# k' of four pairs of token tiles and all of q' as seven products of quarters, with a table for VectorE's and ScalarE's order

## The chip, the cores and the metric

The kernel runs on one core of a Trainium2 chip. The metric is the device time of one execution in microseconds. Before the change three runs took 728.2, 730.2 and 730.42 us; the median is 730.2.

## The reference, cut to what matters

Token matrix `x` is 2048 x 576, in float32. Two branches are mixed by a gate `g` of each token:

```python
g = sigmoid((x * gate_w).sum(-1, keepdims=True))
# branch a: linear attention, 32 heads of 18
q, k, v = split(x @ wqkv)
phi = lambda t: where(t > 0, t + 1, exp(t)) + 1e-6
kv  = einsum("bhsd,bhse->bhde", phi(k), v)
z   = phi(k).sum over tokens
o   = einsum("bhqd,bhde->bhqe", phi(q), kv) / (einsum("bhqd,bhd->bhq", phi(q), z) + 1e-6)
a   = o @ wo
# branch b: real part of a 2-D DFT, by four matrix products
b = Cr @ (x @ Wr.T) - Ci @ (x @ Wi.T)
out = g * a + (1 - g) * b
```

## The kernel before

There are 16 token tiles of 128 rows (`NT`), and 8 pairs of them (tile p and p + 8). A matrix product is done with fp32r operands in three passes: each operand is split in a high part (ScalarE, `hi_of`, L176) and a low part (VectorE, `lo_of`, L186), and TensorE sums high x high, high x low and low x high. The depth of 576 is four chunks of 128 and a rest of 64, whose low part shares a chunk with its high part; so one 128 x 288 half of a tile takes 4 x 3 + 2 = 14 matmuls (`steps`, L272).

The work in order of time:

1. k. Four tiles are done together while the first data arrive (L488 to L503), then twelve one by one in two halves (`k_half`, L452). A raw tile of x is loaded by SP (`load_next`, L256) and split (`split_next`, L262). Each half is turned into its feature by two ScalarE instructions and one of VectorE (`feature`, L341 to L345), and each tile is then split (`k_split`, L462).
2. x'·k, over all tokens, in 5 chunks x 16 tiles (L617 to L672). Into it go the loading and splitting of the token tiles, the sum z, and the product with v (`kv_step`).
3. q, 16 tiles one by one (`q_tile`, L677), the gate's column with them. Between the tiles stand the building of k'v, its product with `wo` to a 576 x 576 matrix M (`build_m`, L762), the moving of M's rows into chunks by DMA from POOL's queue (`move_m`, L771), M's splitting (`split_m`, L787), the division by the denominators (`normalise`, L696) and the forms of the DFT weights (`right`, L402).
4. The transposed q times M, 16 tiles x 2 halves x 14 matmuls (L1109 to L1118).
5. Branch b in two rounds (from 262 us): `Hidden.run`, then `sequence`. Both use Winograd's scheme: a product of 2 x 2 blocks with seven block products instead of eight, on sums of blocks. `PRODUCTS` (L81) says which sum of the left quarters (A22, A11, A12 and four sums, in the order of the code) meets which of the right. The left forms of x are made by `Left` (L352) a few at a time during steps 1 to 4 and stored in DRAM.

Order: TensorE's, VectorE's, ScalarE's and SP's instructions run in the order in which the code issues them (`manual_schedule`; TensorE's order is fixed so only from step 5 on). Every engine waits at the head of its own queue for its data.

Of the kernel before, what the change touches and what calls it, by code (L numbers as in the profile page):

```python
# [8 lines left out]
F = mybir.dt.float32  # L9
# [20 lines left out]


# [3 lines left out]

def gsize(g):  # L50
    return min(GW, D - g * GW)
# [3 lines left out]


# [8 lines left out]

TPAIR = 2 * 7 * HALF * 4
XD = 2 * D * 4
# [6 lines left out]
WH, WL = 5 * HALF * 4, 4 * HALF * 4  # L74
QH = HALF, HALF + 2


LAY_Q = dict(xs=(-256, 4864, 9984, 43776), hi=(15104, 20864), lo=(26688, 31296))
# [3 lines left out]
ORDER = (3, 2, 7, 6, 1, 4, 5)  # L82
MIX_AT = ACC_AT
# [7 lines left out]

# [43 lines left out]
def kernel(  # L135
# [6 lines left out]
    wq: bass.AP,  # L142
    wv: bass.AP,
# [14 lines left out]

    def at(offset, shape, dtype=F, name="t"):
        count[0] += 1  # L160
        t = nc.alloc_sbuf_tensor_at(f"{name}_{count[0]}", list(shape), dtype,
                                    offset=base + offset)
        return t.ap()
# [15 lines left out]
    pending, paced = [], ExitStack()  # L179

# [64 lines left out]
    acc = [at(ACC_AT + i * D * 4, [P, D], F, "acc") for i in range(NT)]  # L245


    raws, split = [], []
    order = []
    xs_ring = Ring(0, 0, 0)  # L250

    def new_xs(name="xs", ring=xs_ring):
        o = ring.next()
        return (at(o, [P, 10, P], R, name), at(o + XS // 2, [P, 5, P], F, "xraw"))

    def load_next():  # L256
        if order:
            xs, raw = new_xs()
            nc.sync.dma_start(out=raw, in_=xa[order.pop(0)])
            raws.append((xs, raw))  # L260
# [8 lines left out]
    def x_at(lay):  # L269
        xs_ring.at, xs_ring.n = [SLOT_AT + o for o in lay["xs"]], 0  # L270
# [10 lines left out]
    def split_wide(t, c, raw):  # L281
        hi_of(t[:, c], raw)
        if c < KC:
            lo_of(t[:, 5 + c], raw, t[:, c])
        else:
            lo_of(t[64:, c], raw[64:], t[64:, c])

    rest_ring = Ring(CONST_AT + 3584, 1184, 2)

    class Wide:  # L290


        def __init__(self, src, lay, start=SLOT_AT, widths=(HALF, HALF)):
            self.src, self.lay, self.got = src, lay, {}
            self.start, self.widths = start, widths

        def load(self, h, pieces=(KC,), queues=None, also=lambda k: None):

            n = self.widths[h]
            cols = slice(h * HALF, h * HALF + n)  # L300
            hi = at(self.start + self.lay["hi"][h], [P, 5, n], R, "wd")
            los, c = [], 0
            for k in pieces:
                o = self.start + self.lay["lo"][h] + c * n * 4
                los.append((c, at(o, [P, k, n], R, "wd"), at(o, [P, k, n], F, "wraw")))
                c += k
            rest = at(rest_ring.next(), [P, n], F, "wraw")
            self.got[h] = hi, los, rest
            queues = queues or [nc.sync] * (len(pieces) + 1)
            for i, (c, _, raw) in enumerate(los):  # L310
                also(i)
                queues[i].dma_start(out=raw, in_=self.src[:, c:c + raw.shape[1], cols])
            also(len(los))
            queues[-1].dma_start(out=rest, in_=self.src[:, KC, cols])

        def split(self, h, n=1, lo_of=lo_of):

            hi, los, rest = self.got[h]
            for c, lo, raw in los:
                k = lo.shape[1]  # L320
                m = max(k * n // KC, 1)
                for a in range(0, k, k // m):
                    cs = slice(a, a + k // m)
                    hs = slice(c + a, c + a + k // m)
                    hi_of(hi[:, hs], raw[:, cs])
                    lo_of(lo[:, cs], raw[:, cs], hi[:, hs])
                    yield
            hi_of(hi[:, KC], rest)
            lo_of(hi[64:, KC], rest[64:], hi[64:, KC])
            yield  # L330

        def row(self, h, j):
            hi, los = self.got[h][:2]
            if j <= KC:
                return hi[:, j]
            return next(lo[:, j - 5 - c] for c, lo, _ in los if c <= j - 5 < c + lo.shape[1])


    es = Ring(Y_AT, 1184, 3)

    def feature(dst, ps):  # L341
        e = at(es.next(), [P, HALF], F, "e")
        nc.scalar.activation(e, ps, AF.Relu, scale=-1.0)
        nc.scalar.activation(e, e, AF.Exp, scale=-1.0)  # L344
        nc.vector.scalar_tensor_tensor(dst, ps, 0.0, e, op0=ALU.max, op1=ALU.add)  # L345


    xforms = [scratch([P, 7, 2, 2 * P], "xm") for _ in range(NP)]
    xrest = scratch([NP * 96, 7 * P], "xr")
    xrest_of = xrest.rearrange("(g q j r) n -> g j r q n", g=2, q=4, j=3)  # L350

    class Left:  # L352

        def __init__(self, k, start, after):
# [922 lines left out]
```

## Time and profile before

| what | value |
|---|---|
| three runs | 728.2, 730.2, 730.42 us |
| span of the profiled execution, first to last instruction | 727.9 us |
| TensorE busy | 723.1 us, 5446 matmuls |
| VectorE busy | 600.3 us, 994 instructions |
| ScalarE busy | 335.5 us, 521 instructions |
| GpSimd busy | 57.1 us, 98 instructions |
| DMA | 158.83 MB, 218 GB/s |

Besides its span, the profiled execution has no time of its own on record; what lies around the span is read from the runs. In the rows, PE is TensorE and PEld its weight loads, DVE is VectorE, ACT is ScalarE, POOL is GpSimd, SP issues DMAs. A row of a group has the line of the code, the engine, the operation, output and inputs with their shapes, the count, then the busy time in us and the mean time of one in ns, then the idle time of the engine just before, with what ended most of it. Many instructions have the line of a helper (L176, L186, L196, L206).

### The profile page before, as it was taken

To read this page: it belongs to the slowest core of one execution; us is meant where nothing else is said; L and a number is where in the kernel's file an instruction comes from. 1 tells how busy PE (TensorE), PEld (TensorE's weight loads), DVE (VectorE), ACT (ScalarE), POOL (GpSimd) and SP (SyncE) were. 2 spreads that over 40 slices of the span, in tenths; PEclk is the share of its full clock that TensorE was granted. 3 is DMA by queue.
4 is the path that set the end of the run, shared out by engine and by line. 5 is a ranking of instruction groups with operands and counts; after the bars stand their busy time and mean duration, and the time that the engine had idled before them with its cause. 6 is when DMAs were issued, how large, how long until landed. Compare 5 with 4: busy or idle time off the path is not lost.

```text
span 727.9 us, 13874 instructions
## 1 busy us (share of the span) xinstructions
PE 723.1 (99%) x5446; PEld 722.0 (99%) x5446; DVE 600.3 (82%) x994; ACT 335.5 (46%) x521; POOL 57.1 (8%) x98
## 2 busy tenths in 40 slices
PE   9999999999999999999999999999999999999997
PEld 9999999999999999999999999999999999999997
DVE  5689877689999948989989989857889988788884
ACT  6898346678643544453434333323435322232330
POOL 1011300051132110000000000000000000000000
PEclk9999999999999999999999999999999999999999
DMA  7376796676477999644475666889954443544440
GB/s 255 91 274 220 266 332 199 221 219 230 147 257 279 365 331 380 182 163 144 147 263 168 225 233 199 306 281 402 377 206 135 168 148 124 163 151 140 152 152 33
DMA packets 54228, 158.83 MB, mean 218 GB/s; under 512 B 6412, under 2 KB 10828, under 8 KB 53140
## 3 DMA queue, kind: packets, MB, share of 16 engines
q1 hardware_dynamic: 44916, 118.90, 48.2%
q0 software_dynamic: 8960, 38.65, 14.6%
q8 instruction: 43, 0.70, 0.4%
q10 hardware_dynamic: 288, 0.41, 0.2%
q14 instruction: 21, 0.17, 0.1%
HBM read 115.06 MB, written 41.39 MB: 215 GB/s over the span
## 4 chain that ended last, share of the span: by engine, by line
PE 99%; DVE 0%; DVEq 0%; issue 0%; POOL 0%; POOLq 0%
PE bank L1051 49%; PE bank L206 23%; PE bank L896 14%; PE bank L626 8%; PE bank L502 2%; PE bank L731 1%; PE bank L232 1%; PE bank L608 0%; DVE row L1067 0%; PE bank L611 0%; DVE ys L196 0%; DVEq L1275 0%; POOL ones_f L228 0%; POOL ident masks.py:197 0%; DVEq L1067 0%
## 5 line engine op out<-in xcount | busy, mean ns | idle before, releaser
L1051 PE MATMUL bank<-fh,c 128*128 128x288 f32 x1792 | 357.4, 295 | 0.0
L1051 PEld LDWEIGHTS bank<-fh,c 128*128 128x128 f32 x1792 | 287.3, 188 | 0.1
L1051 PE MATMUL bank<-fl,c 128*128 128x288 f32 x896 | 264.3, 295 | 0.0
L176 ACT ACTIVATE c<-craw 128x1792 fp32r<-128x1792 f32 (+1 forms) x84 | 121.6, 1447 | 188.2 <-DVE craw L196 167.5
L1051 PEld LDWEIGHTS bank<-fl,c 128*128 128x128 f32 x896 | 168.9, 188 | 0.3
L186 DVE TENSOR_TENSOR c<-craw,c 128x1792 fp32r<-128x1792 f32 (+4 forms) x86 | 142.0, 1654 | 2.8 <-ACT c L176 2.6
L196 DVE TENSOR_TENSOR craw<-craw 128x256 f32<-128x256 f32 (+1 forms) x192 | 98.4, 513 | 24.2 <-DMA craw<-in_ci_dram 12.7
L206 PE MATMUL bank<-wd,xs 128*128 128x288 f32 (+1 forms) x784 | 105.9, 296 | 0.0
L206 PEld LDWEIGHTS bank<-wd,xs 128*128 128x128 f32 x784 | 104.6, 188 | 0.1
L896 PE MATMUL bank<-wf,xf 128*128 128x288 f32 x588 | 91.8, 296 | 0.0
L896 PEld LDWEIGHTS bank<-wf,xf 128*128 128x128 f32 x588 | 84.0, 189 | 0.0
L206 PE MATMUL bank<-mw,qs 128*128 128x288 f32 x448 | 63.2, 297 | 0.0
L626 PE MATMUL bank<-pk,c 128*128 128x288 f32 x448 | 60.8, 296 | 0.0
L206 PEld LDWEIGHTS bank<-mw,qs 128*128 128x128 f32 x448 | 59.9, 188 | 0.2 <-DVE qs L186 0.2
L626 PEld LDWEIGHTS bank<-pk,c 128*128 128x128 f32 x448 | 59.9, 189 | 0.0
L196 DVE TENSOR_TENSOR ys<-bank,ys 128x288 f32<-128x288 f32 x63 | 28.8, 457 | 17.1 <-PE bank L1051 14.0
L345 DVE SCALAR_TENSOR_TENSOR acc<-bank,e 128x288 f32<-128x288 f32 x64 | 28.2, 454 | 17.6 <-ACT e L344 12.2
L186 DVE TENSOR_TENSOR fl<-fl,fh 128x864 fp32r<-128x864 f32 (+1 forms) x32 | 34.7, 1094 | 6.7 <-ACT fh L176 5.4
L176 ACT ACTIVATE fh<-fl 128x864 fp32r<-128x864 f32 (+1 forms) x32 | 29.8, 949 | 16.3 <-DVE fl L196 16.3
L896 PE MATMUL bank<-wf,xr 96*128 96x288 f32 x112 | 33.3, 297 | 0.0
L1116 ACT ACTIVATE acc<-bank,gate 128x288 f32<-128x288 f32 x32 | 16.1, 502 | 35.0 <-PE bank L206 34.8
L196 DVE TENSOR_TENSOR ys<-ys,bank 128x288 f32<-128x288 f32 x47 | 21.2, 450 | 13.0 <-PE bank L1051 12.5
(107 smaller groups left out, 664.8 us busy)
## 6 DMA issues: line engine op xcount, KB each, us to landing
xf<-xm SPq DMA_DIRECT2D x42, 512.0 KB, 8.9
craw<-in_cr_dram SPq DMA_DIRECT2D x32, 512.0 KB, 4.0
craw<-in_ci_dram SPq DMA_DIRECT2D x32, 512.0 KB, 3.5
xraw<-in_xa_dram SPq DMA_DIRECT2D x28, 320.0 KB, 3.4
xm<-xb POOLq DMA_DIRECT2D x8, 1024.0 KB, 6.4
wf<-wm SPq DMA_DIRECT2D x14, 576.0 KB, 5.1
xr<-xr SPq DMA_DIRECT2D x14, 448.0 KB, 8.3
xm<-xb POOLq DMA_DIRECT2D x8, 768.0 KB, 5.8
```

The costliest lines, as they stand in the source:

```text
L176: return nc.scalar.activation(dst, src, AF.Copy, bias=bias)
L186: nc.vector.tensor_tensor(out=dst, in0=src, in1=hi, op=ALU.subtract)
L196: nc.vector.tensor_tensor(out=dst, in0=a, in1=b, op=op)
L206: nc.tensor.matmul(ps, a, b, start=(n == 0), stop=(n == len(pairs) - 1))
L232: nc.tensor.matmul(warm[:, :P], ones_f, ones_f, start=True, stop=True)
L345: nc.vector.scalar_tensor_tensor(dst, ps, 0.0, e, op0=ALU.max, op1=ALU.add)
L502: nc.tensor.matmul(ps[i], x[:, i * P:(i + 1) * P], wkt.row(h, j), start=(c == 0 and n == 0), stop=(c == KC and n == 1))
L626: nc.tensor.matmul(ps[h][:, :HALF], t[:, a, k], pk[s][:, b, half(h)], start=(s == 0 and n == 0), stop=(s == NT - 1 and n == len(passes) - 1))
L731: nc.tensor.transpose(banks[c // KC][:, (c % KC) * P:(c % KC + 1) * P], a, ident)
L896: nc.tensor.matmul(ps, a, b, start=(start and n == 0), stop=(n == len(ops) - 1), skip_group_check=True)
L1051: nc.tensor.matmul(ps[q], c[x][:, l, k], factors[p](y, f), start=(p == 0 and i == 0), stop=(p == NP - 1 and i == 2))
L1116: done.append(nc.scalar.activation(acc[i][:, half(h)], ps[:, :HALF], AF.Copy, scale=gate[:, i:i + 1]))
```

## The change

- k of tile pairs 4 to 7, and q of all eight pairs, are computed as seven products of quarters. A pair's x is a 2 x 2 matrix of quarters (tile p or p + 8; one half of the depth or the other, 256 of 288 rows of it), and so are the weights. A product is 2 chunks x 3 passes = 6 matmuls. The remaining 2 x 32 depth rows are added by two plain matmuls to each of the four outputs. So a pair takes 50 matmuls. k of pairs 0 to 3 stays plain, in two groups of four tiles.
- The left forms of x (`Left`) are those that branch b uses; k, q and branch b now take the same ones. The loads of single x tiles for k and q go away. x's quarters are loaded by SP's queue and no longer by POOL's. Pair 7's forms are read back from DRAM for q, pairs 0 and 1 stay for branch b.
- Sums of products are made in three ways: TensorE adds into a bank into which ScalarE has copied another (`copy`), TensorE goes on in a bank that was copied out, or VectorE adds a bank and a copy (`summed`).
- The order of VectorE's and ScalarE's work is a table, `WHEN`. `slot()` counts up by one after each product, or group of matmuls; a piece of work that was announced with `later` or `plan` is issued in the slot that the table's whole number gives, and within it in the order of the decimals.
- TensorE's order is fixed from the start. The gate's columns go with k's weights.
- M: `build_m`, `move_m` and `split_m` stand between the last q products. Half of the moves go by SP's queue.
- The real DFT weights' forms (`pieces`) stay where branch b reads them; before, they went through DRAM.

The diff, cut:

```diff
+WHEN = {
+    "copy": (
+        19.01, 22.01, 24.01, 25.01, 25.02, 29.01, 31.01, 32.01, 32.02, 36.01, 38.01, 39.01, 39.02,
...
+    "x7": (
+        50.09, 50.10, 50.11, 53.06, 53.05, 53.10, 53.09, 53.12, 53.11, 53.13, 53.07, 56.02),
...
+A22, A11, A12, S4, S3, S2, S1 = range(7)
+LEFTS = {1: A11, 2: A12, 3: S4, 4: A22, 5: S1, 6: S2, 7: S3}
...
+    def later(name, f, n=1, rank=1):
+        i = counts[name] = counts.get(name, -1) + 1
+        t = WHEN[name][i] if name in WHEN else clock[0] + n + rank / 1000
+        assert int(t) > clock[0], (name, i, t, clock[0])
+        planned.setdefault(int(t), []).append((t, f))
...
+    def slot():
+        clock[0] += 1
+        for _, f in sorted(planned.pop(clock[0], ()), key=lambda tf: tf[0]):
+            f()
...
-    def split_next(lo_of=lo_of):
-        if raws:
-            xs, raw = raws.pop(0)
-            hi_of(xs[:, 0:5], raw)
-            lo_of(xs[:, 5:10], raw, xs[:, 0:5])
-            split.append(xs)
...
+        later("relu", lambda: nc.scalar.activation(e, src, AF.Relu, scale=-1.0), n)
+        later("exp", lambda: nc.scalar.activation(e, e, AF.Exp, scale=-1.0), n)
+        later("feature", lambda: nc.vector.scalar_tensor_tensor(
+            dst, src, 0.0, e, op0=ALU.max, op1=ALU.add), n + 1)
...
+        def part(self, n):
+
+            if n < 4:
+                o, a, b, op = ((S1, A22, S4, ALU.add), (S3, A11, S4, ALU.subtract),
+                               (S2, S1, A11, ALU.subtract), (S4, A12, S2, ALU.subtract))[n]
+                add(self.raw(o), self.raw(a), self.raw(b), op)
                 return
...
+            if n % 2:
+                lo_of(lo, raw, hi)
+            else:
+                hi_of(hi, raw)
...
+        def sums(self, b11, b12, b21, b22):
+
+            r = self.low
+            return [lambda: add(r(3), b12, b11, ALU.subtract),
+                    lambda: add(r(5), b22, b12, ALU.subtract),
+                    lambda: add(r(4), b22, r(3), ALU.subtract),
+                    lambda: add(r(6), b21, r(4), ALU.subtract)]
...
+        def rests(self, name, i, h):
+            for a in range(2):
+                nc.tensor.matmul(self.b[name], XR_of[self.p](a, i), self.w.rest[:, h],
+                                 start=False, stop=a == 1, skip_group_check=True)
...
+        def copy(self, name, to):
+            src, pre = self.b["a"], to in "bc" and self.pre
+            if pre:
+                dst = self.b[to] = self.take(to, self.n)
+            else:
+                dst = self.s[name] = at(s_ring.next(), [P, self.n], F, "s")
+            later("copy", lambda: nc.scalar.activation(dst, src, AF.Copy), rank=0)
+
+        def product(self, q):
+            name = {1: "a", 6: "a", 7: "a", 2: "b", 4: "c", 5: "e", 3: "e"}[q]
+            n, x = self.n, X[self.p]
+            start = q in (1, 5) or (q in (2, 4) and not self.pre)
+            if start:
+                self.b[name] = self.take(name, n)
+            if q == 4:
+                self.rests("a", 1, 1)
+                self.copy(4, "s")
+                self.summed(1, 1, self.b["e"], self.s[4])
+            ps, f = self.b[name], PRODUCTS[q][1]
+            ops = [(x(LEFTS[q], a)[:, c * P:c * P + P], self.w(f, c, b))
+                   for c in range(2) for a, b in FULL]
+            for k, (l, r) in enumerate(ops):
+                nc.tensor.matmul(ps, l, r, start=start and k == 0, stop=k == len(ops) - 1,
+                                 skip_group_check=True)
+            if q in (2, 4, 3):
+                self.rests(name, *{2: (0, 0), 4: (1, 0), 3: (0, 1)}[q])
+            slot()
...
+        def summed(self, i, h, ps, s):
+            c = self.out(i, h, self.n if h else HALF)
+            n = self.n if h else HALF
+            later("sum", lambda: add(c, ps[:, :n], s[:, :n]), rank=0)
+            self.eaten(i, h, c, 2)
...
+    jobs = [Job(kind, p, fixed(bases[k % 2])) for k, (kind, p) in enumerate((
+        ("q", 2), ("q", 3), ("k", 4), ("q", 4), ("k", 5), ("k", 6), ("k", 7), ("q", 5), ("q", 6)))]
...
+    order = [(0, 2)]
+    for k in range(len(jobs)):
+        order += [(k, 6), (k, 5), (k, 7)]
+        order += [(k + 1, 1), (k, 4), (k + 1, 2), (k, 3)] if k + 1 < len(jobs) else [(k, 4), (k, 3)]
...
+    load_second()
+    load_x(2, 0)
+    load_wq()
+    load_x(3, 1)
+    load_x(4, 2)
+    XR_parts[4] = load_x_rest(4, 2)
+    pace(mybir.EngineType.PE)
...
+    for p, s, r, k in ((5, 0, 0, key(0, 6)), (6, 1, 1, key(1, 6)), (7, 2, 2, key(3, 6)),
+                       (0, 0, None, key(7, 6)), (1, 1, None, 2)):
+        at_step(k, load_x, p, s)
...
+    ends = [Job("q", p, lambda name, n: bank()[:, :n], False) for p in (1, 0, 7)]
...
     def move_m(g):
-
-
         row, end = g * GW, g * GW + gsize(g)
+        queues = [nc.gpsimd, nc.sync]
         while row < end:
...
-                nc.gpsimd.dma_start(out=mraw[p:p + k, c], in_=src)
+                queues[g % 2].dma_start(out=mraw[c // 2][p:p + k, c % 2], in_=src)
...
-    def split_m(h):
-        hi_of(mhi[:, :KC, half(h)], mraw[:, :, half(h)])
-        lo_of(mlo[:, :, half(h)], mraw[:, :, half(h)], mhi[:, :KC, half(h)])
...
+    def split_m(h, k):
+        cs = slice(2 * k, 2 * k + 2)
+        hi, lo, raw = mhi[:, cs, half(h)], mlo[k][:, :, half(h)], mraw[k][:, :, half(h)]
+        return lambda: hi_of(hi, raw), lambda: lo_of(lo, raw, hi)
...
+    at_step(first_c[0], kv_step, 4)
+    at_step(first_c[0], build_kv)
+    for g in range(NG):
+        at_step(first_c[5 + g], build_m, g)
+        at_step(first_c[7 + g], move_m, g)
```

The slots run so: 1 to 10 are the first four tiles' chunks, 11 to 19 the next four tiles (and one product of quarters), 20 to 82 the products of k's four pairs and q's pairs 2 to 6, with the first token tiles from 80 on, up to 122 x'·k, up to 143 q's pairs 1, 0 and 7, and up to 176 the transposed q times M.

More of the change, by code (lines that the diff above doesn't have):

```diff
@@ L490 @@
-        parts = wkt.split(h, KC)
+        n = GATED[h]
+        ps = [banks[4 * h + i][:, :n] for i in range(FT)]
         for c, (raw, hi, lo) in enumerate(first):
@@ new lines @@
+            if h == 1 and c < FT:
+                t = TILES[c]
+                feature(kraw[t][:, half(0)], banks[c][:, :HALF])
+            slot()
+            did((h, c))
+    firsts = ps
+    for k in range(2 * FT):
+        h, i = divmod(k, FT)
+        n = GATED[h]
+        if k == 2 * FT - 1:
+            jobs[0].product(1)
+        ps = banks[k][:, :n]
+        ops = []
+        for c in range(5):
+            _, hi, lo = second[c]
+            ops += [(x[:, i * P:(i + 1) * P], wk_row(h, j, n))
+                    for x, j in ((hi, c), (hi, 5 + c), (lo, c))[:3 if c < KC else 1]]
+            if c == KC:
+                ops.append((lo[:, i * P:(i + 1) * P], wk_row(h, c, n)))
+        run(ps, ops)
+        slot()
+        if h == 0:
+            t, end = TILES[k], firsts[k]
+            feature(kraw[t][:, half(1)], end[:, :HALF],
+                    gated=(gate[:, t:t + 1], end[:, HALF:HALF + 1]))
+        t = TILES[FT + i]
+        feature(kraw[t][:, half(h)], ps[:, :HALF],
+                gated=(gate[:, t:t + 1], ps[:, HALF:HALF + 1]) if h else None)
+        did(("p", k))
```

1013 lines of the change are left out of this document (590 added, 423 removed), and 40 rows, old and new, of the table WHEN.

## The prediction

> **What bounds the kernel now.** I read the page first, then the chain of waits in order of time, TensorE's own waits, the groups by form, and stages by window. In the page, the busy times and the chain:
>
> ```profile
> span 727.9 us, 13874 instructions
> PE 723.1 (99%) x5446; PEld 722.0 (99%) x5446; DVE 600.3 (82%) x994; ACT 335.5 (46%) x521; POOL 57.1 (8%) x98
> PE 99%; DVE 0%; DVEq 0%; issue 0%; POOL 0%; POOLq 0%
> ```
>
> TensorE is the chain. TensorE's waits have one row, and the chain in order of time shows the stages (start, length, what):
>
> ```profile
> PE bank L232 <- POOL ones_f L228: 1.2, 1, 1.2
> 4.86 15.11 PE bank L502 x112
> 19.97 44.55 PE bank L206 x336
> 83.70 0.12 PE bank L608
> 84.67 12.85 PE bank L626 x96
> 262.03 52.52 PE bank L896 x392
> 721.12 0.47 DVE ys L196
> ```
>
> From 4.86 to 721.1 TensorE never waits for anything, so what is saved is the number of matmuls times the time of one, and what can be lost is a wait that does not exist today. One plain matmul is 44.55 / 336 = 132.6 ns; one in the quarter products of the later stage (L896, seven to a product, some of 96 rows) is 52.52 / 392 = 134.0 ns. The first 262 us are the part that changes. There the cover is this (columns: window, then busy us and count of TensorE, weight loads, VectorE, ScalarE, GpSimd; clock, DMA share, GB/s):
>
> ```profile
> 0.00:10.00 10.00, 8.80 (x57) 8.63 (x58) 5.01 (x10) 6.05 (x12) 1.76 (x11) 1.00 0.85 291
> 10.00:20.00 10.00, 10.00 (x78) 10.00 (x77) 6.40 (x13) 6.36 (x16) 1.46 (x2) 1.00 0.46 173
> 40.00:60.00 20.00, 20.00 (x153) 20.00 (x153) 17.71 (x32) 17.89 (x38) 3.16 (x6) 1.00 0.78 274
> 60.00:80.00 20.00, 20.00 (x153) 20.00 (x152) 17.64 (x32) 13.30 (x25) 3.04 (x5) 1.00 0.78 279
> 180.00:240.00 60.00, 60.00 (x464) 59.92 (x463) 58.28 (x119) 32.32 (x72) 13.36 (x21) 1.00 0.66 226
> 0.00:262.00 262.00, 260.80 (x1976) 260.32 (x1977) 212.15 (x415) 167.59 (x357) 47.73 (x84) 1.00 0.70 241
> ```
>
> VectorE is the second engine: 88% busy from 40 to 80 us, 97% from 180 to 240, and yet nothing of TensorE's waits for it.
>
> **The change, part by part.** *Matmuls.* Now every tile of k and q takes 2 x 14 matmuls, 56 for a pair of tiles. As seven products of quarters a pair takes 7 x 6 plus 4 x 2 for the remaining rows, 50. Twelve pairs change (four of k, eight of q): 72 matmuls fewer, 72 x 132.6 ns = **-9.5 us**. The 600 that take the new form I price at L896's rate, 1.4 ns more each: **+0.8**. If they run as plain ones it is 0. The two gate columns move from q's half (224 matmuls) to k's (312): 88 x 2 columns x 0.46 ns (132.6 / 288) is below 0.1. The Trainium skill ("TensorE: Matmul & The Clock Gate", Back-to-back issue gap) gives N/2.4 + 2.5 ns for a warm matmul, 122.5 ns here; the saving would be an estimated 8.8 by it. The trace has 132.6, so it does not agree, and the row counts.
>
> *VectorE and ScalarE.* What one instruction costs, by its form:
>
> ```profile
> L345 DVE SCALAR_TENSOR_TENSOR acc<-bank,e 128x288 f32<-128x288 f32 x64 | 28.2, 454 | 17.6 <-ACT e L344 12.2 <-DMA xr<-xb 5.3
> L186 DVE TENSOR_TENSOR xs<-xraw,xs 128x640 fp32r<-128x640 f32 x28 | 23.0, 823 | 1.0 <-ACT xs L176 0.8 <-PE bank L206 0.2
> L196 DVE TENSOR_TENSOR xb<-xb 128x256 f32<-128x256 f32 x36 | 14.3, 422 | 0.3
> L464 DVE SCALAR_TENSOR_TENSOR pk<-acc,pk 128x576 fp32r<-128x576 f32 x16 | 12.0, 755 | 1.9 <-ACT pk L176 1.5
> L196 DVE TENSOR_TENSOR fl<-bank,y 128x288 f32<-128x288 f32 x48 | 21.7, 452 | 6.4 <-PE bank L896 6.3
> L921 ACT ACTIVATE y<-bank 128x288 f32<-128x288 f32 x16 | 6.5, 407 | 11.8 <-PE bank L896 11.8
> L186 DVE TENSOR_TENSOR xs<-xs,xs 128x512 fp32r<-128x512 f32 x5 | 3.5, 691 | 0.8 <-ACT xs L176 0.8
> ```
>
> Removed: the 28 splits of x tiles (23.0 us of VectorE), most of the 32 small gate operations, 16 small copies that go to ScalarE. Added: 30 sums of banks (30 x 0.452 = 13.6 us), 48 copies out of banks on ScalarE (48 x 0.407 = 19.5), eight sums of the weights' quarters (576 columns, 8 x 0.755 = 6.0) and about 5 us more of their low parts. VectorE's total hardly moves; its place does. The forms of x, made a few per tile until now, are needed before the first product, so the table's early slots are full. Back to back, instructions overlap (VectorE's timeline: start, length):
>
> ```profile
> 42.21 0.46 DVE L345 SCALAR_TENSOR_TENSOR acc<-bank,e 128x288 f32<-128x288 f32 x1
> 42.58 0.75 DVE L464 SCALAR_TENSOR_TENSOR pk<-acc,pk 128x576 fp32r<-128x576 f32 x1
> 43.24 0.46 DVE L345 SCALAR_TENSOR_TENSOR acc<-bank,e 128x288 f32<-128x288 f32 x1
> ```
>
> The next one starts 0.09 us before the last one's end. Counting the table up to slot 82 (the end of the products of k and six pairs of q): 34 of 256 columns, 75 of 288, 32 of 512, 53 of 576 and two others, 196 instructions: 34 x 0.422 + 75 x 0.454 + 32 x 0.691 + 53 x 0.755 + 0.9 = 111.3, less 196 x 0.09 = **93.7 us of VectorE**. TensorE has 690 matmuls there, 690 x 0.133 = **91.8 us**. Up to slot 105: 268 instructions, 154.4 - 24.1 = 130.2, against 962 matmuls and two steps of k'v of 0.97 us (83.70 to 84.67), 129.9. So VectorE becomes TensorE's equal for 130 us. ScalarE is about as full: 107.3 us in 233 instructions up to slot 82, 86.4 with the overlap, and 50 pairs of relu and exp, where the second waits for the first, add some 0.11 each.
>
> What saves it is distance. For each product I set VectorE's summed work up to the form that it reads against TensorE's summed work up to the product. The form is ready 6 to 13 us ahead in nearly all, 3.9 us at the narrowest (pair 7's first form, slot 53, read in slot 59); for the token tiles of slots 94 to 112 it is 3.6 to 4.4. Late by 93.7 - 91.8 = 1.9 us plus some tenths from the start, VectorE stays inside that. Term: 0, bounds 0 and 2.0. The leads are what hides it; without them all of the 2.0 would show.
>
> *Loads at the start.* SP now issues all early loads. Up to the first sum of q's weights (slot 9, at 4.9 + 12.5 = 17.4 us) these are 1.3 MB of x, 1.5 of k's weights, 1.3 of the second x block, 0.5 of pair 2 and 0.6 of q's, 5.2 MB. At 291 GB/s from about 2 us on they land at 20, 2.6 late; slots 11 to 14 hold 3.4 us of VectorE against 7.4 of TensorE and take that up. At 173 GB/s after 10 us it is 23.3, so 1.9 past that cushion. Term 0, bounds 0 and 1.9. Loads of pairs that moved from POOL's queue to SP's stand behind waits for a slot of x to come free; behind them are only later pairs and the token tiles, which are read 20 slots on.
>
> *The move of M'.* It goes from a stretch of seven q tiles to slots 131 to 136. The moves and their readers now (the first row is of the DMA issues, the others of the tiles' views: ns min/median/max, first and last start):
>
> ```profile
> mraw<-mf POOLq DMA_DIRECT2D x4, 252.0 KB, 4.9
> L176 ACT ACTIVATE mw<-mraw x4: 427/788/1150, 173.0 to 177.7; 128x1152 fp32r<-128x1152 f32 x2, 128x288 fp32r<-128x288 f32 x2
> L783 POOL DMA_DIRECT2D mraw<-mf x1: 665/665/665, 159.1 to 159.1; - x1
> L206 PE MATMUL bank<-mw,qs x448: 288/295/399, 194.6 to 261.7; 128*128 128x288 f32 x150
> ```
>
> A move lands in 4.9 us; the last are issued from 159.1 on, the first split is at 173, and the first matmul on it at 194.6. In the table a split stands two slots behind the eviction that it needs: 1.6 us of products and 1.6 of M' matmuls for the first, so 1.7 us late; about 3.7 us of ScalarE's own work for the last rows, 1.2 late. Behind that wait on ScalarE stand the relu and exp of the last q pairs, for whose banks TensorE waits. ScalarE has 24.3 + 1.2 us in slots 122 to 143, TensorE 156 + 40 matmuls, 25.7. So nearly all of 2.9 could reach TensorE, or none if ScalarE is ahead. Between 0 and 2.9 I take the middle, **+1.5**.
>
> *Sum.* -9.5 + 0.8 + 1.5 = -7.2 on the profiled span of 727.9, 720.7. The median of the runs, 730.2, is 2.3 above that span (the lowest run, 728.2, is 0.3 above), so **723.0**.
>
> **Rivals.** (1) *VectorE paces the first 105 slots a little.* In its rows from 40 to 80 us it idles 11.6%, mostly behind ScalarE:
>
> ```profile
> DVE acc L345 <- ACT e L344: 12.2, 19, 1.8
> ```
>
> With half that idle share, 130.2 / 0.942 = 138.2, 8.3 behind TensorE's 129.9, less the 3.6 lead: +4.7, 727.7, no change to speak of. For: orders on both engines are fixed, and each waits for the other. Against: 97% was reached from 180 to 240.
>
> (2) *Slower: VectorE is the bound.* With the whole 11.6%, 130.2 / 0.884 = 147.3; 17.4 behind, less 3.6, +13.8: 736.8. It decides once idle passes about 3.6 + 7.2 = 10.8 us of the 130. For: the same rows. Against: that idle is of an engine nobody waited for. The Trainium skill ("VectorE: DVE Perf Modes", The DRAIN you can't avoid) says the next operation is not started until the pipe is empty; then the full 154.4 would count, an estimated 744. The three timeline rows above disagree (0.37 us from start to start for a 0.46 us instruction), which is why this is no likelier.
>
> (3) *Loads pace the start.* At 173 GB/s x's pair 3 lands 4 us after VectorE could take it, and about 3 of these reach TensorE: 726.0. Against: 291 GB/s at 85% share in the first window.
>
> **How the numbers follow.** Forecast 0.60, own range 719 to 726; rival 1 0.17, rival 2 0.13, rival 3 0.10. The low end is 730.2 - 9.5 without a wait, 720.7, less the spread of the runs shown, about 2; the high end takes in rival 3, rival 1 and the bounds of the waits together: 719 to 730. A difference under 0.3%, 2.2 us, cannot be told from none. Faster: 0.60 + 0.10 + half of rival 1, 0.78; same: 0.10; slower: 0.12.
>
> **What would show it.** TensorE with 72 matmuls fewer, and the first of the later stage's L896 matmuls near 254 us in place of 262. Right if its waits sum to under 3 us and stand near the M' splits; wrong if waits for VectorE sum to 10 us between 15 and 125 us (rival 2), or waits for loads appear before 45 us (rival 3). Windows of VectorE from 20 to 120 us should be over 95% busy; under 90% with TensorE waiting is rival 1 or 2. A product's matmul at other than 132 to 134 ns would upset the first two terms.

## The result, and the profile after

The changed kernel takes 722.7 us, the median of four runs (722.2 to 723.5), beside 729.35 of the kernel before in its four (728.2 to 730.4). The ratio is 0.991, with a 95% interval of 0.989 to 0.9925. The forecast was 723.0. The profiled execution has a time of its own of 722.17, of which 720.5 is span; the span forecast was 720.7.

The page's first rows, and the slices of VectorE and ScalarE, of the changed kernel:

```profile
span 720.5 us, 13712 instructions
PE 714.2 (99%) x5374; PEld 712.1 (99%) x5374; DVE 591.1 (82%) x997; ACT 341.1 (47%) x598; POOL 47.8 (7%) x90
DVE  6999998927997248899998899857889888778884
ACT  6988993229766335353334234313535233332330
```

TensorE has 72 matmuls fewer, 5374 for 5446, and is still 99% busy. TensorE's waits, in the view of waits (what waited and for what: us in all, times, longest), have one row more than before, this one:

```profile
PE bank L748 <- DVE acc L334: 0.8, 1, 0.8
```

The chain in order of time (start, length, what) tells the stages. First the changed kernel, then the two rows of the kernel before that the prediction did not show:

```profile
15.02 5.12 DMA wd<-in_wq_dram
45.18 3.19 PE bank L748 x24
256.01 52.52 PE bank L1215 x392
308.53 177.12 PE bank L1367 x1344
485.64 52.34 PE bank L1215 x392
537.98 175.38 PE bank L1367 x1320
```

```profile
314.54 178.47 PE bank L1051 x1344
545.35 175.75 PE bank L1051 x1320
```

The first row is the load of q's weights: in the changed kernel the chain begins with loads, up to 20.1 us, and goes by work of VectorE and ScalarE to 41 us, where TensorE takes over; TensorE itself loses little there, as the next rows show. L1215 is the line that was L896, and L1367 the one that was L1051. The part that changed ends at 256.0 in place of 262.0: **6.0 us** of the 7.4 by which the spans differ. The other 1.4 is nearly all in the first sequence, 177.12 for 178.47, whose code is not touched; the experiments return to it.

Inside the first 256 us the windows are (columns as in the prediction):

```profile
0.00:10.00 10.00, 8.66 (x48) 8.43 (x49) 3.62 (x8) 4.76 (x9) 1.59 (x10) 1.00 0.81 279
20.00:40.00 20.00, 20.00 (x151) 19.87 (x150) 19.94 (x42) 18.45 (x53) 4.44 (x8) 1.00 0.54 205
40.00:60.00 20.00, 19.93 (x148) 19.47 (x147) 20.00 (x45) 17.98 (x47) 5.39 (x11) 1.00 0.81 300
60.00:80.00 20.00, 20.00 (x150) 19.85 (x149) 19.96 (x44) 18.24 (x52) 3.22 (x6) 1.00 0.62 222
80.00:100.00 20.00, 19.88 (x147) 19.36 (x146) 19.80 (x38) 19.97 (x51) 0.00 (x0) 1.00 0.29 82
180.00:200.00 20.00, 19.22 (x147) 18.79 (x146) 18.96 (x39) 14.75 (x40) 9.55 (x16) 1.00 0.46 136
```

VectorE is at 99% or more from 20 to 100 us, and ScalarE at about 90% or more, 99.9% at the end. Yet TensorE loses little: 148 matmuls from 40 to 60 us, where the kernel before had 153, and 147 from 180 to 200 us, where it had 154.

How much is lost can be added up from the trace: the time from the start of one matmul to the start of the next, less 132.5 ns for one of 288 columns, summed over the first part. Before, the sum is 3.4 us; after, 6.5. So **3.1 us** of waits are new. By place they are 0.9 in the first 10 us, 0.6 from 40 to 50, 0.5 (0.75, less 0.26 that was there before) from 80 to 90, 1.1 (1.27, less 0.2) from 180 to 190, and nowhere else more than 0.35. The timeline (all engines) names the one at 41 us (start, length, what, idle time before it):

```profile
40.48 0.63 ACT L298 ACTIVATE xb<-xb 128x512 fp32r<-128x512 f32 x1
41.02 0.39 ACT L732 ACTIVATE bank<-bank 128x288 f32<-128x288 f32 x1
41.46 0.30 PEld L715 LDWEIGHTS bank<-wd,xs 128*128 128x128 f32 x2 [0.31 <-ACT bank L732]
```

and the one at 186 us:

```profile
185.39 0.76 DVE L949 SCALAR_TENSOR_TENSOR pz<-acc,zb 128x576 f32<-128x576 f32 x1
186.06 0.68 DVE L324 TENSOR_TENSOR qs<-bank,qs 128x512 fp32r<-128x512 f32 x1
186.66 0.45 DVE L334 TENSOR_TENSOR acc<-bank,s 128x288 f32<-128x288 f32 x1
187.17 1.07 PE L748 MATMUL bank<-wd,xq 128*128 128x288 f32 x6 [0.78 <-DVE acc L334]
```

At 41 us the rests (L715, the plain matmuls of the remaining rows) wait for ScalarE's copy into their bank (L732): between product 7, whose bank is copied out, and the rests that write the copy there is one product, 0.8 us, and ScalarE was busy with a piece of x (L298) until the copy. At 186 us a product waits for a bank that VectorE still has to sum (L334); ahead of that sum stand a `pz` (L949) and a low part of q (L324), 1.3 us. Before these, from 182.3 us on, VectorE's row holds three low parts of M' (L324) and two features, one behind the other: the splitting of M' takes part in this delay, as work.

### The profile page after: what moved, and what is told of

It is laid out like the page before. It is cut to its first block, busy times and chain, and to the rows that moved or that the text cites. A ratio compares the mean times of both kernels' runs of the same rounds, so it can differ in the third digit from the quotient of the medians.

```text
span 720.5 us, 13712 instructions
## 1 busy us (share of the span) xinstructions
PE 714.2 (99%) x5374; PEld 712.1 (99%) x5374; DVE 591.1 (82%) x997; ACT 341.1 (47%) x598; POOL 47.8 (7%) x90
## 4 chain that ended last, share of the span: by engine, by line
PE 91%; DVE 3%; DMA 3%; ACT 1%; issue 1%; SPq 0%; DVEq 0%; ACTq 0%
PE bank L1367 49%; PE bank L1215 15%; PE bank L344 9%; PE bank L1001 8%; PE bank L748 7%; DMA xs<-in_xf_dram 2%; PE bank L715 2%; PE bank L1057 1%; DMA wd<-in_wq_dram 1%; DVE acc L402 1%; ACT pk L298 1%; DVE xb L324 0%; PE bank L977 0%; DVE wd L324 0%; DVE xb L334 0%
## 5 line engine op out<-in xcount | busy, mean ns | idle before, releaser
L1367 PE MATMUL bank<-fh,c 128*128 128x288 f32 x1792 | 356.0, 295 | 0.0
L1367 PEld LDWEIGHTS bank<-fh,c 128*128 128x128 f32 x1792 | 287.1, 188 | 0.0
L1367 PE MATMUL bank<-fl,c 128*128 128x288 f32 x896 | 263.8, 294 | 0.0
L298 ACT ACTIVATE c<-craw 128x1792 fp32r<-128x1792 f32 x64 | 109.0, 1704 | 167.9 <-DVE craw L334 167.9
L1367 PEld LDWEIGHTS bank<-fl,c 128*128 128x128 f32 x896 | 168.8, 188 | 0.0
L324 DVE TENSOR_TENSOR c<-craw,c 128x1792 fp32r<-128x1792 f32 (+2 forms) x66 | 129.3, 1962 | 0.4 <-ACT c L298 0.2
L334 DVE TENSOR_TENSOR craw<-craw 128x256 f32<-128x256 f32 (+1 forms) x192 | 98.3, 512 | 25.2 <-DMA craw<-in_ci_dram 14.1
L1215 PE MATMUL bank<-wf,xf 128*128 128x288 f32 x588 | 91.8, 296 | 0.0
L1215 PEld LDWEIGHTS bank<-wf,xf 128*128 128x128 f32 x588 | 83.9, 189 | 0.0
L748 PE MATMUL bank<-wd,xb 128*128 128x288 f32 (+1 forms) x462 | 69.9, 296 | 0.0
L748 PEld LDWEIGHTS bank<-wd,xb 128*128 128x128 f32 x462 | 64.3, 189 | 0.3 <-ACT s L732 0.2
L334 DVE TENSOR_TENSOR ys<-bank,ys 128x288 f32<-128x288 f32 x63 | 28.8, 457 | 16.3 <-PE bank L1367 12.6
L324 DVE TENSOR_TENSOR fl<-fl,fh 128x864 fp32r<-128x864 f32 (+1 forms) x32 | 34.6, 1093 | 6.7 <-ACT fh L298 5.4
L298 ACT ACTIVATE fh<-fl 128x864 fp32r<-128x864 f32 (+1 forms) x32 | 29.8, 949 | 16.3 <-DVE fl L334 16.3
L1215 PE MATMUL bank<-wf,xr 96*128 96x288 f32 x112 | 33.3, 298 | 0.0
L1389 ACT ACTIVATE ys<-bank 128x288 f32<-128x288 f32 x16 | 6.6, 411 | 53.0 <-PE bank L1367 53.0
L334 DVE TENSOR_TENSOR fl<-bank,e 128x288 f32<-128x288 f32 x45 | 20.3, 451 | 12.6 <-PE bank L1215 12.6
L334 DVE TENSOR_TENSOR ys<-ys,bank 128x288 f32<-128x288 f32 x47 | 21.1, 450 | 11.1 <-PE bank L1367 10.4
## 6 DMA issues: line engine op xcount, KB each, us to landing
c<-in_xg_dram SPq DMA_DIRECT2D x20, 256.0 KB, 3.2
```

Of the source, the lines that this page charges most:

```text
L298: return nc.scalar.activation(dst, src, AF.Copy, bias=bias)
L324: nc.vector.tensor_tensor(out=dst, in0=src, in1=hi, op=ALU.subtract)
L334: nc.vector.tensor_tensor(out=dst, in0=a, in1=b, op=op)
L748: nc.tensor.matmul(ps, l, r, start=start and k == 0, stop=k == len(ops) - 1, skip_group_check=True)
L1215: nc.tensor.matmul(ps, a, b, start=(start and n == 0), stop=(n == len(ops) - 1), skip_group_check=True)
L1367: nc.tensor.matmul(ps[q], c[x][:, l, k], factors[p](y, f), start=(p == 0 and i == 0), stop=(p == NP - 1 and i == 2))
```

## The experiments

All edits are to the changed kernel. Beside the medians I compare the start of the first L1215 matmul, the end of the part that the change touches; it does not see what the later part does.

**The changed kernel again.** No edit.

> The changed kernel unchanged, as the base of the others. My theory: TensorE paces it, so about 722.7 us again, its first L1215 matmul near 256 us. Of the 7.4 us that the span lost, 6.0 lie before that point and 1.4 in the later stage, which the change does not touch; if those 1.4 are a difference between executions and not of the change, the later stage here takes anything between the two (177.1 to 178.5 us for its first 1344 matmuls). If the change causes them, 177.1 again.

722.5 us (721.25 to 724.5), ratio 0.991 [0.990, 0.993]. The first L1215 starts at 255.58, so two executions of one kernel differ by 0.4 there. The wait of 0.8 for the sum is there again, and from there to the end of the span it is 465.2 us, beside 464.5 in the first execution and 465.9 before. In the kernels below, whose later part has the same code, it is 463.9 to 468.7, and the first sequence takes 177.12 us in four of them and 178.80 in another. The 1.4 us are of the size by which executions differ; I do not count them to the change.

The 0.4 at L1215 are made in the first 10 us. Added up as above, over the matmuls of 288 columns alone, the excess there is 1.0 us in the first execution, 0.6 in the repeat and 0.1 before the change. Every execution profiled here starts at half rate, with matmuls of 128 columns 213 ns apart; the trace's clock record has full rate from 6.3 us on in the first execution, from 5.2 in the repeat and from 4.1 before the change, where the 128 columns then stand 112 ns apart. In the first execution three matmuls of k, from 5.4 to 6.2 us, therefore stand 240 ns apart. In the kernels below full rate starts between 4.5 and 7.3 us, so some tenths at L1215 can come from this alone.

**No rests.** The 72 matmuls of the remaining rows in the jobs of slots 19 to 83 are left out, and their part of k and q is missing.

```diff
-            for a in range(2):
+            for a in range(0 if self.pre else 2):
```

> Leaves out the 72 matmuls of the remaining depth rows in the nine product jobs of slots 19 to 83; nothing else of the order changes. If TensorE alone paces that stretch: 72 x 0.1326 = 9.5 us less, 713.2. If VectorE paces it as well (it is over 99% busy from 20 to 100 us in the changed kernel): VectorE's summed work stays 93.7 us against then 82.3 of TensorE, and after its lead of about 4 us is used up TensorE waits for it: 3 to 5 us less, 718 to 720, with waits of TensorE for VectorE or ScalarE that add to 5 us or more between 60 and 110 us.

722.3 us (720.95 to 726.3), ratio 0.992 [0.990, 0.994]. The first L1215 starts at 254.43: of another 9.5 us of matmuls, **1.15** comes through. TensorE's waits, and its window from 40 to 60 us:

```profile
PE bank L748 <- ACT s L732: 2.6, 5, 0.7
PE bank L748 <- DVE acc L334: 1.1, 3, 0.5
PE bank L748 <- ACT bank L732: 0.6, 3, 0.3
```

```profile
40.00:60.00 20.00, 18.20 (x124) 16.54 (x124) 20.00 (x44) 17.38 (x46) 5.45 (x11) 1.00 0.84 304
```

A pair now takes 42 matmuls, so 124 are 2.95 pairs in 20 us; before the edit it was 148 of 50, 2.96. The pairs go no faster. The next limit lies right behind TensorE. The edit also brings a copy and its reader nearer together, though, so it does not say whether that limit is an engine's work or the distance.

**No sum of z.** Fourteen of the fifteen additions of k' into z are left out (14 of 0.75 us, some 10 us of VectorE; z is wrong by it).

```diff
-    plan("z", *(lambda a=a, t=t: add(zacc, a, kraw[t][:, :D])
-                for a, t in zip([kraw[TILES[0]][:, :D]] + [zacc] * (NT - 2), TILES[1:])))
+    plan("z", lambda: add(zacc, kraw[TILES[0]][:, :D], kraw[TILES[1]][:, :D]),
+         *(lambda: None for _ in range(NT - 2)))
```

> Leaves out 14 of the 15 additions that sum z (14 x 0.665 = 9.3 us of VectorE, slots 42 to 78). If TensorE paces the stretch: 0 to 1 us less, only what the small waits there were worth. If VectorE paces it: 5 to 9 us less.

722.5 us, ratio 0.991 [0.990, 0.992], and the first L1215 starts at 255.58, to the hundredth where it did in the repeat.

```profile
60.00:80.00 20.00, 20.00 (x151) 19.92 (x150) 14.92 (x35) 18.45 (x51) 3.22 (x6) 1.00 0.60 214
```

VectorE fell from 99.8% to 75% in this window, and TensorE did 151 matmuls in place of 150. So VectorE at 99.8% was **not** pacing the kernel there. The left-out additions stand from 60 us on (in the repeat's trace the first of them is at 60.1); from 40 to 60 us VectorE is 100% busy here too, and of that stretch the run says nothing.

**Sum of z twice.** The same fourteen additions are made twice (z is wrong by it).

```diff
+    def z_twice(a, t):
+        add(zacc, a, kraw[t][:, :D])
+        if a is zacc:
+            add(zacc, a, kraw[t][:, :D])
+
-    plan("z", *(lambda a=a, t=t: add(zacc, a, kraw[t][:, :D])
+    plan("z", *(lambda a=a, t=t: z_twice(a, t)
```

> Does each of these 14 additions twice (14 x 0.79 = 11.1 us more of VectorE in slots 42 to 78; the second waits for the first). If VectorE is level with TensorE and some 4 to 6 us ahead at the reads, as the sums say: 5 to 7 us more, 728 to 730. If VectorE has idle time to spare there: 0 to 1 us more. If it already paces: 11 us more, 734.

731.6 us (731.2 to 734.4), ratio 1.004 [1.003, 1.0055]; the first L1215 at 265.40, 9.8 later for 11.1 us of work.

```profile
PE bank L748 <- DVE acc L334: 5.0, 4, 1.7
PE bank L748 <- ACT s L732: 1.5, 3, 0.9
PE bank L715 <- ACT bank L732: 1.0, 1, 1.0
```

The leads of 4 to 6 us by which I had let VectorE fall behind were hardly there: nearly all of the added work came out at the end. What TensorE waits for are sums that free banks (`acc`), not the forms whose leads I had worked out.

**Part of the sum of z twice.** Four of the fourteen additions twice, 3.2 us more (z is wrong by it).

```diff
...
+        if a is zacc and t in TILES[2:6]:
+            add(zacc, a, kraw[t][:, :D])
...
```

> Does only four of the z additions twice: 4 x 0.79 = 3.2 us more of VectorE, in slots 46 to 60. All fourteen twice, 11.1 us, cost 9.1. If VectorE has a fixed spare of 2.0 us: 1.2 us more than the changed kernel. If the cost is in proportion: 2.6 us more. If the leads take it: 0.

725.4 us (725.0 to 725.95), ratio 0.993 [0.992, 0.995]: 2.9 over the repeat's median. The first L1215 starts at 258.98, 3.4 later; 0.5 of that is the longer half rate at the start of this execution (an excess of 1.1 in the first 10 us, the repeat's 0.6). So about 2.9 of the 3.2 come out, and hardly any spare shows. Fewer sums gain nothing, and a few more cost nearly all that they take: from 60 us on VectorE and TensorE are level.

**Rests twice.** The 72 matmuls are made two times (that part of k and q counts double).

```diff
-            for a in range(2):
+            for k in range(4 if self.pre else 2):
+                a = k % 2
```

> Does the 72 matmuls of the remaining rows in slots 19 to 83 twice (those rows count double), so that products and their copies stand further apart and no engine but TensorE has more to do. If TensorE sets the pace there: 72 x 0.1326 = 9.5 us more, less the small waits of about 1.9 us between 30 and 90 us that the greater distance covers: 7.6 to 9.5 us more than the changed kernel. If VectorE or ScalarE sets it: 0 to 4 us more. Leaving these matmuls out gave only 1.2 us ahead of L1215; the difference of the two is what the distance and the other engines held back.

732.05 us (732.0 to 734.5), ratio 1.004 [1.002, 1.006]; the first L1215 at 264.59, **9.0** later for 72 x 132.6 ns = 9.5.

```profile
40.00:60.00 20.00, 20.00 (x151) 19.83 (x150) 18.17 (x39) 15.97 (x40) 4.29 (x8) 1.00 0.76 275
```

With 72 more, VectorE goes down to 91% and TensorE is at its full rate. So 72 matmuls are worth 9.0 us on the way to where the changed kernel stands, and 1.2 on the way beyond it. It stands at the bend.

**Every second relu twice.** ScalarE makes 26 of the first 52 relus again, with the same result (8.6 us).

```diff
...
+            for _ in range(2 if i < 52 and i % 2 else 1):
+                nc.scalar.activation(e, src, AF.Relu, scale=-1.0)
...
```

> Does every second relu of the first 52 twice: 26 x 0.33 = 8.6 us more of ScalarE, spread over slots 7 to 82. If ScalarE is level with TensorE there (91.9 us against 91.8): 5 to 8 us more. If it has time to spare: 0 to 2 us more.

728.85 us (727.4 to 729.6), ratio 0.998 [0.997, 0.999]; the first L1215 at 261.69, 6.1 later. Of ScalarE's 8.6 us all but 2.5 shows, and TensorE names it:

```profile
PE bank L754 <- ACT s L738: 3.1, 6, 0.8
```

**Two or three reliefs at once.** No rests together with no sum of z; no rests together with the first 52 exp left out (24 us of ScalarE, gates and features wrong by it); and all three.

```diff
-            for a in range(2):
+            for a in range(0 if self.pre else 2):
...
-    plan("z", *(lambda a=a, t=t: add(zacc, a, kraw[t][:, :D])
-                for a, t in zip([kraw[TILES[0]][:, :D]] + [zacc] * (NT - 2), TILES[1:])))
+    plan("z", lambda: add(zacc, kraw[TILES[0]][:, :D], kraw[TILES[1]][:, :D]),
+         *(lambda: None for _ in range(NT - 2)))
```

> Leaves out the 72 matmuls of the remaining rows in slots 19 to 83 and also 14 additions of z (9.3 us of VectorE). Leaving out the matmuls alone took 1.2 us off the part ahead of L1215. If VectorE took over there, relieving it lets most of the 9.5 us through: 6 to 9 us less than the changed kernel. If ScalarE is level too (91.9 us of work up to slot 82 with its relu-exp pairs, against 82.3 of TensorE then): 1 to 3 us less, and TensorE's waits name ScalarE.

723.7 us (720.5 to 724.3), ratio 0.991 [0.989, 0.9935]; the first L1215 at 254.55. Nothing more than without the rests alone. The waits turn to ScalarE's copies:

```profile
PE bank L748 <- ACT s L732: 4.1, 9, 0.7
PE bank L748 <- DVE acc L334: 0.7, 2, 0.5
```

```diff
-            for a in range(2):
+            for a in range(0 if self.pre else 2):
...
-        later("exp", lambda: nc.scalar.activation(e, e, AF.Exp, scale=-1.0), n)
+        i = counts.get("exp", -1) + 1
+        later("exp", (lambda: None) if i < 52 else
+              lambda: nc.scalar.activation(e, e, AF.Exp, scale=-1.0), n)
```

> Leaves out the same 72 matmuls and the first 52 exponentials (about 0.35 to 0.47 each with the wait for relu, 18 to 24 us of ScalarE, slots 7 to 82); z stays whole. If ScalarE alone took over: 6 to 9 us less than the changed kernel. If VectorE is level as well (93.7 us against 82.3): 1 to 3 us less, and TensorE's waits name VectorE.

723.2 us (722.5 to 725.5), ratio 0.992 [0.990, 0.994]; the first L1215 at 254.43, again nothing more. Now VectorE is named:

```profile
PE bank L750 <- DVE acc L334: 2.7, 6, 0.7
PE bank L750 <- ACT bank L734: 1.6, 4, 0.6
```

```diff
-            for a in range(2):
+            for a in range(0 if self.pre else 2):
...
-        later("exp", lambda: nc.scalar.activation(e, e, AF.Exp, scale=-1.0), n)
+        i = counts.get("exp", -1) + 1
+        later("exp", (lambda: None) if i < 52 else
+              lambda: nc.scalar.activation(e, e, AF.Exp, scale=-1.0), n)
...
-    plan("z", *(lambda a=a, t=t: add(zacc, a, kraw[t][:, :D])
-                for a, t in zip([kraw[TILES[0]][:, :D]] + [zacc] * (NT - 2), TILES[1:])))
+    plan("z", lambda: add(zacc, kraw[TILES[0]][:, :D], kraw[TILES[1]][:, :D]),
+         *(lambda: None for _ in range(NT - 2)))
```

> Leaves out all three: the 72 matmuls, 14 additions of z and 52 exponentials. If the three engines are level in slots 19 to 83, only this lets the 9.5 us of the matmuls through: 8 to 10 us less than the changed kernel, about 713. If loads or the copies' places in the order hold TensorE there, it stays at 717 or more.

719.95 us (718.7 to 721.6), ratio 0.987 [0.986, 0.989].

```profile
251.14 52.53 PE bank L1217 x392
```

```profile
PE bank L750 <- DVE acc L334: 1.4, 3, 0.5
PE bank L750 <- ACT s L734: 0.7, 2, 0.4
PE bank L750 <- ACT bank L734: 0.5, 2, 0.3
```

Only with all three relieved does the part end earlier by more than 1.2 us: by 4.4 against the repeat. That is still under half of the 9.5. Two windows tell where the rest stays:

```profile
40.00:60.00 20.00, 18.60 (x127) 16.93 (x126) 20.00 (x45) 14.91 (x39) 5.61 (x11) 1.00 0.84 304
60.00:80.00 20.00, 19.55 (x139) 18.52 (x138) 16.87 (x38) 17.13 (x45) 2.96 (x6) 1.00 0.58 208
```

The full rate is 151 matmuls in 20 us. From 40 to 60 us TensorE makes 127, but there VectorE is 100% busy, as the additions left out stand after 60 us: no run has relieved VectorE ahead of that, so its work stays a possible limit there. From 60 to 80 us VectorE and ScalarE have time, and TensorE still makes 12 fewer; its waits for sums and copies are 0.25 to 0.5 us each on average. I read these as the distance from a product to the copy or sum that its bank needs, which the missing rests made shorter. No run has lengthened that distance alone, so it is argued and not shown, and so is how much of the five microseconds it holds. From the first L1217 to the end of the span it is 468.7 us in this execution, the slowest of the four, beside the repeat's 465.2. Of these 3.5, 2.1 are in the first sequence (179.96 for 177.90 to the start of the second round), and 1.4 in the second round, where VectorE waits 2.5 for a load.

**Eight places of the table moved.** Nothing is left out; eight pieces of VectorE's and ScalarE's work stand one to four slots later, out of the way of copies and sums that TensorE waited for (an exp and its relu, the high and low part of a piece of k and of x, a norm, a low part of q). The lines of two of them:

```diff
-        146.09, 139.07, 147.05, 148.08, 148.11, 148.14, 150.07, 150.09, 151.05, 152.09, 152.10,
+        146.09, 143.07, 147.05, 148.08, 148.11, 148.14, 150.07, 150.09, 151.05, 152.09, 152.10,
...
-        141.04, 142.06, 144.07, 144.08, 146.05, 146.07, 148.06, 148.07, 150.05, 150.06, 152.05,
+        142.05, 142.06, 144.07, 144.08, 146.05, 146.07, 148.06, 148.07, 150.05, 150.06, 152.05,
```

> The changed kernel with seven places of the table moved: four pieces of ScalarE go behind the copies that TensorE waits for at 41, 48 and 82 us, and of VectorE one product of the normaliser and one low part of the transposed q go behind the sum that it waits for at 186 us. Nothing is left out. If each wait is the order alone, these waits of 0.25, 0.15, 0.3 and 0.8 us go: 1 to 1.5 us less. If the engines' fullness only moves the waits on: 0 to 0.5 less, or more.

721.9 us (721.4 to 723.15), ratio 0.990 [0.989, 0.992]. The part ends at 254.46, 1.1 before the repeat:

```profile
254.46 52.52 PE bank L1215 x392
```

TensorE's waits have no row for a sum any more, and from 180 to 200 us it has 154 matmuls where the changed kernel had 147. The wait at 186 us came from the order of VectorE's work, and the two pieces shown (a norm and a low part of q) were what was moved there. Added up as above, its waits are 5.0 us, where the changed kernel has 6.5: 0.8 less from 180 to 190 and 0.4 less from 40 to 50, as meant, 0.3 more from 50 to 60, and 0.7 less in the first 10 us, where nothing was moved and full rate came 1.5 us earlier. The median is 0.6 below the repeat's, and the intervals don't tell that from nothing; it is the fastest of the kernels that compute everything.

**No table for the gates and features.** The four groups gate, relu, exp and feature go out of the table, so that each is issued in the first slot after its product.

```diff
-    "exp": (
-        6.03, 7.04, 9.02, 9.03, 13.02, 14.07, 13.03, 15.21, 14.05, 15.13, 15.04, 17.06, 16.03, 17.03,
...
-    "relu": (
-        6.01, 7.01, 8.01, 9.01, 12.01, 14.04, 13.01, 15.16, 14.03, 15.10, 15.01, 17.04, 16.01, 17.01,
...
```

> Takes the features' four groups (gate, relu, exp, feature) out of the table: each is issued in the first slot after its product, ahead of the other work of that slot. Nothing is left out. The forms that the next products read then stand behind features that nobody waits for yet; their leads of 4 to 8 us shrink by the features brought forward, some 3 to 5 us of each engine. If the leads are what hides VectorE: 2 to 6 us more. If not: 0 to 1 us.

753.6 us (751.1 to 754.7), ratio 1.031 [1.029, 1.033]; far beyond what was expected.

```profile
287.18 52.52 PE bank L1194 x392
```

```profile
PE bank L727 <- ACT s L711: 21.0, 10, 3.0
ACT bank L711 <- PE bank L727: 10.6, 13, 1.4
DVE acc L313 <- ACT s L711: 8.0, 6, 2.6
```

```profile
60.00:80.00 20.00, 15.38 (x100) 14.90 (x100) 15.39 (x33) 13.23 (x35) 3.75 (x7) 0.91 0.58 219
100.00:120.00 20.00, 15.06 (x102) 14.59 (x101) 15.79 (x29) 16.36 (x39) 0.00 (x0) 0.93 0.27 81
```

The work is the same, and no engine is busy for more than 82% of these windows: TensorE waits for ScalarE's copy, VectorE too, ScalarE for TensorE. One of the longest waits in the timeline:

```profile
51.62 0.44 ACT L379 ACTIVATE e<-acc 128x288 f32<-128x288 f32 x1 [1.13 <-DVE acc L313]
52.44 0.39 ACT L711 ACTIVATE s<-bank 128x288 f32<-128x288 f32 x1
52.89 0.54 PE L727 MATMUL bank<-wd,xb 128*128 128x288 f32 x2 [2.68 <-ACT s L711]
```

A relu (L379) has to wait for its sum, and the copy (L711) that stands behind it and its exp holds TensorE. So the 31.6 us hang on the order. In these windows the granted clock falls, to 0.91 and 0.93, where the windows shown of the changed kernel have 1.00. Some 5 of the 31.6 us come by this way: the trace has four stretches of 3.4 us at a clock of 0.50, with 48 matmuls 230 to 245 ns apart in place of 132.5.

## Why the prediction came out, and where it was wrong

**The matmuls, -9.5: right.** 5374 for 5446 are the 72, and the rests made twice cost 9.0 for the same number. The section of the Trainium skill that the prediction holds against the row of 132.6 ("TensorE: Matmul & The Clock Gate", Back-to-back issue gap) gives that formula for an isolated matmul and says that a stream with weight loads goes otherwise; so the row does not contradict it.

**The new form, +0.8: too much.** 24 matmuls of a product run in 3.19 us, 132.9 ns each, the plain ones' 132.6 and not L896's 134.0. By this row 600 cost 0.2.

**The move of M', +1.5: the place about right, the mechanism wrong.** The changed kernel's view of the tile:

```profile
L298 ACT ACTIVATE mw<-mw x4: 670/684/685, 178.1 to 183.1; 128x576 fp32r<-128x576 f32 x4
DMA to landing us min/median/max: 1.7/2.6/2.8
```

The moves land in 2.6 us, not 4.9, and no split waits for one. TensorE's new wait is right there, 0.8 us at 186 and 1.1 with what follows it, but it is for a sum that stands behind other work of VectorE's, M's low parts among it. The term came near by chance.

**VectorE level, term 0: right; the reason, wrong.** The counts said equal by slot 82, and so it is: above 99% in three windows of four from 20 to 100 us, and 99.0% in the last; nothing gained without 10 us of its work from 60 us on, 9.8 lost with 11 more. But I said that leads of 3.9 to 13 us would hide a delay. With 3.2 us added, about 2.9 came out. I had measured leads of the forms of x, and the handoffs that gave way are shorter ones: a copy or a sum that frees a bank for a product one or two slots on.

**ScalarE: not in the sum.** The text had its 86 us up to slot 82, plus 50 pairs at 0.11, beside TensorE's 91.8, and went on with VectorE alone. With 8.6 us more it costs 6.1, so it is level within 2.5, and its copies made the waits at 41 and 48 us and one at 82: about 1.1 us that no term held. Of the 3.1 us these are the second part; the third is the 1.1 around 186. The first is the 0.9 of the first 10 us, at rival 3's place but much smaller than its 3; about 0.4 of it is no wait but the matmuls at half rate.

**The sum.** So the steps read -9.5 + 0.2 + 3.1 = -6.2, and k's first matmul starts 0.2 later (5.06 for 4.86): 6.0, as measured, where I had -7.2. The whole came out at 7.4 since the later part was 1.4 shorter in the profiled execution. In the medians the fall is 6.7 in place of 7.2, and the median before is 729.35, 0.85 under the one that the forecast started from; these two nearly cancel. So a part of the closeness is luck: about a microsecond. Of the signs that the prediction named, the first L1215 near 254 is at 256.0, and the waits, to be under 3 us and near the splits of M', are 3.1 with only 1.1 there.

**The rivals.** VectorE pacing by 4.7 us and VectorE the bound by 13.8 are both contradicted by the kernel without z's sum, which is not faster. The 11.6% of idle time on which they stood was VectorE's waiting for work, not a share of its time that it needs: it is 0.1% from 40 to 80 us now that work is there. The estimated 744 us took the Trainium skill ("VectorE: DVE Perf Modes", The DRAIN you can't avoid) at its word that the next operation does not start until the pipe is empty; but the same section says that a next operation that is not held starts earlier. The rows at 186 us, where an instruction of 0.76 us is followed after 0.67, and the measured 722.7 go with that exception. Loads at the start cost about 0.5, not 3; q's weights land at 20.1 us (the row of 15.02), as counted at 291 GB/s.

**What the prediction did not ask.** Where the next matmul saved would go. The kernel stands at a bend: 72 more cost 9.0 us, 72 less save 1.2, and relieving TensorE together with one of the other two (VectorE from 60 us on) saves no more than that.

## What to carry to other kernels

When the bounding engine is 99% busy, set the sum of the next two engines' work beside its own, slot by slot, before crediting a saving: it pays up to the point where they are level, and here by an eighth beyond it. List the shortest handoffs (a copy or a sum that frees a bank for the next product) and not only the long leads of inputs, because small delays come through at the shortest one. Where engines are level, the written order of the work decides more than its amount: the same instructions in a simple order cost 31 us, a part of it by a lower clock.

## What the runs showed of the hardware that was not expected

- After a wait TensorE loses more than the wait. Eleven times in the first part of the changed kernel, after its half-rate start, two matmuls are 236 to 241 ns from start to start in place of 132.5, some 105 ns more, among them those right behind the waits at 41, 48, 82 and 186 us. The trace fits a reading by the weight loads: in the steady rows a weight load starts some 260 ns ahead of its matmul; behind the wait at 41 us load and matmul start 2 ns apart, and the next load starts 108 ns after that.
- Every execution profiled here starts at half rate: the trace's clock record has full rate from 4.1 us on in the one before and from 4.5 to 7.3 us in the others.
- The moves of M' landed in 2.6 us when half of them were issued by SP and half by GpSimd, in place of 4.9 by GpSimd alone. Whether the halving does it is not tested: GpSimd's own half lands in 2.7 us now, and before the change its queue also carried loads of weights between the moves.
- The untouched first sequence has two rates in these executions: in the start-to-start times of its matmuls, without the 50 longest and 50 shortest, the mean is 131.8 to 132.1 ns in eleven of the fourteen and 132.6 to 132.8 in three (before, without rests and z, without all three). That is about 1.1 us of the 1.4 between the two executions first compared. What selects one is open.
- The granted clock was 0.91 and 0.93 in the two windows shown of the kernel without the table, where TensorE's listed waits for ScalarE are 2.1 us on average and 3.0 at the longest. The Trainium skill ("TensorE: Matmul & The Clock Gate", Part 1: The HAM clock gate) puts the drop to half the clock behind an idle window of about 3.4 us; here no listed wait is as long as that, and in the 3.4 us ahead of the four stretches at 0.50 TensorE was busy for 0.85 to 1.5 us, so it was not idle for the whole of such a window:

```profile
58.33:61.74 3.41, 1.49 (x13) 1.26 (x11) 3.04 (x7) 2.73 (x8) 0.83 (x2) 1.00 0.68 262
61.74:65.15 3.41, 3.41 (x14) 3.41 (x15) 2.73 (x6) 0.98 (x3) 1.31 (x3) 0.50 0.73 281
```
